# A fused attention + SwiGLU kernel: normalization of rows 5 to 7 reordered, one activation turn moved behind others, four transfers cut differently

## The chip, the cores and the metric

The kernel runs on one core of a Trainium2 chip. The metric is the device time of one execution in microseconds (us); the number given for a kernel is the median of several runs. The engines have short names in the profile: PE is the matrix engine (PEld its weight loads), DVE the vector engine, ACT the scalar engine, POOL the general one, and SP only issues transfers (its rows are SPq). Every engine works through its own list of instructions in order and waits on semaphores for the others. Transfers are issued by SP or ACT and carried by 16 DMA engines.

## The reference

Inputs are x (2048 tokens of 576 features), the attention weights wqkv (576 x 1728) and wo (576 x 576), and the feed-forward weights w_gate, w_up (576 x 4608) and w_down (4608 x 576), all bf16.

```python
xn = (x - mean(x)) / sqrt(var(x) + 1e-5)          # per token, over the 576 features
q, k, v = split(xn @ wqkv)                        # 32 heads of 18
# each token attends to itself and the 7 tokens 2, 4, ... 14 before it
attn = softmax over these 8 of (q . k) * 18**-0.5 # positions before the start get -1e9
o = sum over the 8 of attn * v
out = x + o @ wo + (silu(xn @ w_gate) * (xn @ w_up)) @ w_down
```

## The kernel before

**Tiling.** The 2048 tokens are seen as 16 rows of 128: partition p holds tokens 16p to 16p+15, and "row r" is the token r of every partition. A shift by 2 tokens is then mostly a shift by 2 rows on the same partition. The program has a first phase that makes q, k and v of the 16 rows, and then four token groups tt of four rows each, every one with nine chunks of gate and up matmuls (line 562) and the down and output projections (line 591). The attention itself is vector work, cut into pieces that a small planner (`Filler`) lays between the gate and up chunks.

**Names in the profile.** Several buffers share memory, and the profile prints the owner's name. The x rows (`xc_b`) and the normalized rows (`xn_b`, two buffers: rows 0-3 and 8-11 use the first, 4-7 and 12-15 the second) lie in the not yet needed `wd`, so `wd<-wd,mv,rstd` is a normalization. The qkv weights and the staged k and v (`stage`) lie in `hT`. `xnT` holds the normalized rows with the features on the partitions, which is what the matmuls read; "turning" a row means making its part of `xnT`.

**Normalizing a row** takes five steps: `ln_stats` (two BATCH_NORM_STATS2 and an aggregate on DVE, lines 210-211), `ln_sqrt` (ACT, 216), `ln_recip` (DVE, 221) and `ln_apply` (DVE, subtract and multiply at 226, and a copy of the last 64 features at 229, which a 64-row matmul needs twice). `ln_apply(8)` overwrites the place of row 0 and therefore waits until the transfer that turns row 0 has landed.

**Turning a row.** Rows 1 to 4 are turned on PE: `turn(r)` puts ten small transposing matmuls (263) into the matmul list of the row before, behind its 24th or 28th of 36 matmuls, and ACT and DVE each copy half of the result to `xnT` (267). Rows from 5 on are turned by a transposing transfer that SP issues (`transp_dma`, 271). Row 0 is needed in plain form at the very start and is turned a second time, as the others, by `transp_dma(0)` for the gate and up matmuls.

**The matmuls of a row** (`p_row`, 281) are 36, in 18 pairs of half-height tiles that run side by side, into four PSUM banks. `p_evac` copies the four banks out on ACT in six pieces (344); `between` puts an `ln_sqrt` before piece `last`. The banks of row r are used again by row r+2. Pieces 1, 2, 4 and 5 write `stage`; rows 8-11 write the buffers that rows 0-3 used, after SP's `move(0)` (356 to 359: halo copies into the rings `Kr` and `Vr`) has read them.

**Order on SP in the first phase:** loads, the two small ring fills (494), the turns of rows 5, 0, 6, 7, 8, 9, then `move(0)`, the turns of rows 10 to 13, `move(1)` with two `store`s, the turns of rows 14 and 15, then the second gate and up chunk. SP issues them strictly one after another. From row 4 on, the loop issues for each row r its matmuls, its evacuation, then `ln_sqrt`, `normalize` of rows 2r and 2r+1 and the statistics of the next two.

**The end.** Row 15 is the last output row. Its residual is added by a matmul, so its two halves are only copied from PSUM, one by ACT and one by DVE, and each engine's half is sent by a transfer of its own (606-607).

Of the kernel before, what the change touches and what calls it, by code (L numbers as in the profile page):

```python
# [20 lines left out]
HALF = D // 2  # L21
# [8 lines left out]
R = 16  # L30
RT = 4
# [39 lines left out]
def kernel(  # L71
# [11 lines left out]
    nc = tc.nc  # L83
# [6 lines left out]
    x_v = A_x.rearrange("b (p r) d -> p (b r) d", r=R)  # L90
    out_v = out.rearrange("b (p r) d -> p (b r) d", r=R)
# [26 lines left out]
    xr = big.tile([P, RT, D], bf16, name="xr")  # L118
    kv_d = dram.tile([2, NTT - 1, P, RT * D], bf16, name="kv_d")
# [3 lines left out]
    XC, XN = RT * D, RT * DPAD  # L123
# [9 lines left out]
    stage = [hTf[:, o + i * XC:o + (i + 1) * XC].rearrange("p (r d) -> p r d", d=D) for i in range(4)]  # L133
# [55 lines left out]
    def load_wd(ch):  # L189
        nc.sync.dma_start(wd[:, ch * FC:(ch + 1) * FC, :],  # L190
                          B_w_down[ch * FC * P:(ch + 1) * FC * P, :].rearrange("(f p) j -> p f j", p=P))
# [7 lines left out]
    def ln_open(c):  # L199
        mv = lns.tile([P, 4, 2], f32, name="mv")  # L200
        rstd = lns.tile([P, 4], f32, name="rstd")
        ln[c] = (xc_b[c], xn_b[c % 2], mv, rstd)

    def ln_stats(r, n=1):
        c, j = divmod(r, 4)
        xc, xn, mv, rstd = ln[c]
        for i in range(j, j + n):
            stats = lns.tile([P, 2, 6], f32, name="stats")
            for k in range(2):
                nc.vector.bn_stats(stats[:, k, :], xc[:, i, k * HALF:(k + 1) * HALF])  # L210
            nc.vector.bn_aggr(mv[:, i, :], stats[:].rearrange("p c s -> p (c s)"))  # L211

    def ln_sqrt(r, n=1):
        c, j = divmod(r, 4)
        xc, xn, mv, rstd = ln[c]
        nc.scalar.activation(rstd[:, j:j + n], mv[:, j:j + n, 1], ACT.Sqrt, bias=eps_t[:], scale=1.0)  # L216

    def ln_recip(r, n=1):
        c, j = divmod(r, 4)
        rstd = ln[c][3]  # L220
        nc.vector.reciprocal(rstd[:, j:j + n], rstd[:, j:j + n])

    def ln_apply(r, lo=0, hi=D):
        c, j = divmod(r, 4)
        xc, xn, mv, rstd = ln[c]
        nc.vector.tensor_scalar(xn[:, j, lo:hi], xc[:, j, lo:hi], mv[:, j, 0:1], rstd[:, j:j + 1],  # L226
                                op0=ALU.subtract, op1=ALU.mult)
        if hi == D:
            nc.vector.tensor_copy(xn[:, j, D:DPAD], xn[:, j, 512:D])  # L229
# [39 lines left out]
    def transp_dma(r):  # L269
        c, j = divmod(r, 4)  # L270
        nc.sync.dma_start_transpose(xnT[:, :, r * P:(r + 1) * P], ln[c][1][:, j, :])
# [12 lines left out]
    def p_row0(between):  # L284
        t = [new_ps("qkv_ps") for g in range(NG)]
        for kt in range(4):
            for g in range(NG):
                p_mm(t, g, kt, None, 0, kt == 0, False)
            if kt == 2:
                between()  # L290
        for i in range(2):
            for half in range(2):
                p_mm(t, i + 2 * half, 4, half, 0, False, True)
        return t
# [9 lines left out]
    def p_row(r, between=None, at=(0, 1)):  # L304


        t = [None] * NG
        fence = {}
        for swap in range(2):
            for i in range(2):  # L310
                kts = (0, 1, 2, 3) if swap else (0, 4, 1, 2, 3)
                for kt in kts:
                    for half in range(2):
                        g = i + 2 * (half ^ swap)
                        if t[g] is None:
                            t[g] = new_ps("qkv_ps")
                        mm = p_mm(t, g, kt, half, r, swap == 0 and kt == 0, swap == 1 and kt == 3)
                        if swap == 0 and kt == 3 and half == 1:
                            fence[i] = fence_after(mm)
                        if swap and kt == 0 and half == 0:  # L320
                            fence_before(mm, fence[i])
                    if swap and (i, kt) == at and between is not None:
                        between()
        return t

    def p_evac(r, t, only=range(6), between=None, last=6):


        c, j = divmod(r, 4)
        ks, vs = stage[2 * c % 4], stage[(2 * c + 1) % 4]  # L330
        vdst = vs[:, j, :].rearrange("p (d h) -> p d h", h=H)
        parts = [
            (QO[:, r, 0:G], t[0][:, 0:G]),
            (ks[:, j, HALF:D], t[2][:, 0:HALF]),
            (vdst[:, :, 0:8], t[2][:, HALF:G].rearrange("p (h d) -> p d h", d=DH)),
            (QO[:, r, G:D], t[1][:, 0:D - G]),
            (ks[:, j, 0:HALF], t[1][:, D - G:G]),
            (vdst[:, :, 8:H], t[3][:, 0:G].rearrange("p (h d) -> p d h", d=DH)),
        ]
        for n in only:  # L340
            if n == last:
                between()
            if r:
                nc.scalar.copy(*parts[n])  # L344
            elif n < 5:
                nc.scalar.mul(*parts[n], ln[0][3][:, 0:1])
            else:
                nc.vector.tensor_scalar(*parts[n], ln[0][3][:, 0:1], None, op0=ALU.mult)
# [9 lines left out]
        if c == 0:  # L358
            nc.sync.dma_start(ring[:, HALO:HALO + RT, :], st)

    def store(m, c):
        st = stage[(2 * c + m - 1) % 4]
        nc.sync.dma_start(kv_d[m - 1, c - 1], st.rearrange("p r d -> p (r d)"))

    def ring_load(m, tt):
        ring = Kr if m == 1 else Vr
# [85 lines left out]
    def normalize(r, n=1):  # L452
        ln_recip(r, n)
        for i in range(r, r + n):
            ln_apply(i)
            if i > 4:
                transp_dma(i)

    def turn(r):
        return lambda: transp_halves(r)  # L460
# [20 lines left out]
    t = p_row0(first)  # L481
# [6 lines left out]

    t = p_row(1, turn(2), (0, 3))
    ln_stats(3)  # L490
    p_evac(1, t, range(6), lambda: ln_sqrt(3), 4)
    normalize(3)
    for ring in (Kr, Vr):
        nc.sync.dma_start(ring[0:1, 0:HALO, :], wz[0:1, :].unsqueeze(1).to_broadcast([1, HALO, D]))

    t = p_row(2, turn(3))
    ln_open(1)
    ln_stats(4)
    p_evac(2, t, range(6), lambda: ln_sqrt(4), 3)
    normalize(4)  # L500
    ln_stats(5)

    t = p_row(3, turn(4))
    ln_sqrt(5)
    normalize(5)
    transp_dma(0)
    ln_stats(6, 2)
    p_evac(3, t)
    ln_sqrt(6, 2)
    normalize(6, 2)  # L510
    ln_open(2)
    ln_stats(8, 2)

    for r in range(4, R):
        t = p_row(r)
# [82 lines left out]
    def d_out(r, sub, t):  # L598
        ot = tmp.tile([P, D], bf16, name="ot", tag="ot", bufs=3)
        for h in range(2):  # L600
            cols = slice(h * HALF, (h + 1) * HALF)
            if r < R - 1:
                nc.vector.tensor_tensor(ot[:, cols], t[h][:, 0:HALF], xr[:, sub, cols], op=ALU.add)  # L603
                continue
            copy, eng = ((nc.scalar.copy, nc.scalar), (nc.vector.tensor_copy, nc.sync))[h]
            copy(ot[:, cols], t[h][:, 0:HALF])  # L606
            eng.dma_start(out_v[:, r, cols], ot[:, cols])
        if r < R - 1:
            nc.sync.dma_start(out_v[:, r, :], ot[:])

    for tt in range(NTT):
        for ch in range(NCH):
            it = tt * NCH + ch
            for p in range(2):
                g_pair(tt, ch, p)
                for j in (2 * p, 2 * p + 1):
                    g_evac(ch, j)
                    if it % NCH < NCH - 1 or p == 0:
                        dve.pump(1.4)
            if ch == NCH - 1:  # L620
                dve.drain(lambda: chains[0] > tt)
                for r in range(RT * tt, RT * tt + RT):
                    nc.sync.dma_start_transpose(oT[:, :, r * P:(r + 1) * P], QOP[:, r, :])
            if it + NSLOT < NTT * NCH:
                load_gu(it + NSLOT)
            if tt == 0:
                if 1 <= ch <= 7:
                    load_wd(ch - 1)
                for _ in range(3 if ch in (1, 2) else 2):
                    if wo_order:  # L630
                        load_wo(wo_order.pop(0))
                if ch == 0:
                    store(2, 3)
            if ch == 7:
                nc.sync.dma_start(xr[:], x_v[:, RT * tt:RT * tt + RT, :])
            if ch == 1 and tt < NTT - 1:
                chain(tt + 1)
        for sub in range(0, RT, 2):
            t, fence = {}, {}
            for swap in range(2):  # L640
                for i in (sub, sub + 1):
                    d_half(tt, i, swap, t, fence)
                    if swap:
                        dve.pump(12.5 if i == sub else 4.0)
                        d_out(RT * tt + i, i, t[i])
# [30 lines left out]
```

## Time and profile before

Three runs: 504.74 us median (504.69 to 504.84).

| what | value |
| --- | --- |
| time of the profiled execution | 504.91 us |
| its span, first to last instruction | 503.1 us |
| granted PE clock | 0.999 |
| PE busy | 497.4 us, 99% of the span |
| DVE busy | 328.8 us, 65% |
| ACT busy | 200.9 us, 40% |
| first phase, row matmuls (line 281) on the chain that ended last | 9% of the span |
| gate and up matmuls (562) on it | 56% |
| down and output matmuls (591) on it | 32% |

PE is the engine that sets the time: the chain that ended last runs through it for 96% of the span. Anything on another engine costs time only where PE has to wait for it, so the places to look for are the few short stretches in which PE is idle. The profiled execution is 0.17 us above the median of the runs.

### The profile page before, as it was taken

How to read it: one execution, taken by the hardware profiler on the slowest of the kernel's cores; microseconds unless marked ns; L12 is line 12 of the kernel's file. 1: busy time of each engine (PE TensorE's matmuls, PEld its weight loads, DVE VectorE, ACT ScalarE, POOL GpSimd, SP SyncE). 2: the span in 40 equal slices, each digit the busy share in tenths (PEclk: the TensorE clock that was granted, in tenths of full speed). 3: DMA queues.
4: the chain of work that ended last, by engine and by line, in shares of the span. 5: the costliest groups of instructions: out<-in, count | busy, mean ns of one | idle time of the engine just before them, and what ended most of it. 6: DMA issues, size and time to landing. Idle time of an engine off the chain costs nothing.

```text
span 503.1 us, 13262 instructions
## 1 busy us (share of the span) xinstructions
PE 497.4 (99%) x5799; PEld 283.4 (56%) x5799; DVE 328.8 (65%) x479; ACT 200.9 (40%) x416; POOL 0.7 (0%) x6
## 2 busy tenths in 40 slices
PE   8999999999999999999999999999999999999997
PEld 4555544444677644444777544445777444446775
DVE  5787598898999698999898139995980222221001
ACT  4756657754400255554300445557000444553000
POOL 0000000000000000000000000000000000000000
PEclk9999999999999999999999999999999999999999
DMA  8979988788921046536720054465500335553100
GB/s 311 251 198 247 293 293 272 227 266 261 236 88 61 25 129 200 187 104 228 150 85 38 28 185 149 135 189 156 136 25 14 107 113 172 166 165 40 27 14 25
DMA packets 76466, 75.42 MB, mean 150 GB/s; under 512 B 22628, under 2 KB 72192, under 8 KB 76408
## 3 DMA queue, kind: packets, MB, share of 16 engines
q1 hardware_dynamic: 75976, 73.91, 49.5%
q8 instruction: 45, 0.74, 0.6%
q10 hardware_dynamic: 432, 0.66, 0.4%
q14 instruction: 13, 0.11, 0.1%
HBM read 58.76 MB, written 5.90 MB: 129 GB/s over the span
## 4 chain that ended last, share of the span: by engine, by line
PE 96%; DMA 2%; DVE 1%; SPq 0%; ACT 0%; issue 0%
PE g_ps L562 56%; PE d_ps L591 32%; PE qkv_ps L281 9%; DMA hT<-in_A_wqkv_dram 1%; DMA xnT<-wd 1%; DVE stats L210 0%; DVE wd L226 0%; SPq L148 0%; ACT rstd L216 0%; PE pt L263 0%; DVE ot L606 0%; DVE mv L211 0%; ACT xnT L267 0%; SPq L144 0%; DVE wd L229 0%
## 5 line engine op out<-in xcount | busy, mean ns | idle before, releaser
L562 PE MATMUL g_ps<-xnT,gu 64*128 64x512 bf16 x2592 | 280.4, 376 | 0.0
L562 PEld LDWEIGHTS <-gu 64*128 64x128 bf16 x2592 | 126.1, 94 | 152.9
L573 ACT ACTIVATE sg<-g_ps 128x512 bf16<-128x512 f32 x144 | 87.3, 606 | 156.6 <-PE g_ps L562 156.6
L591 PE MATMUL d_ps<-wd,hT 64*128 64x288 bf16 x2304 | 146.4, 283 | 0.0
L591 PEld LDWEIGHTS <-hT 64*128 64x128 bf16 x2304 | 112.0, 94 | 29.8
L575 DVE TENSOR_TENSOR hT<-sg,uc 128x512 bf16<-128x512 bf16 x144 | 60.2, 419 | 93.5 <-ACT uc L574 93.2
L393 DVE TENSOR_REDUCE PP<-PP 128x64 f32<-128x1152 bf16 x64 | 84.9, 1347 | 0.4
L574 ACT CAST uc<-g_ps 128x512 bf16<-128x512 f32 x144 | 85.2, 592 | 0.0
L281 PE MATMUL qkv_ps<-hT,xnT 64*128 64x432 bf16 x540 | 50.3, 343 | 0.5 <-DMA xnT<-wd 0.5
L388 DVE TENSOR_TENSOR PP<-QO,Kr 128x2304 bf16<-128x2304 bf16 (+1 forms) x35 | 43.5, 1251 | 8.3 <-DMA Kr<-hT 8.1
L603 DVE TENSOR_TENSOR ot<-d_ps,xr 128x288 bf16<-128x288 f32 x30 | 12.3, 451 | 51.0 <-PE d_ps L591 51.0
L420 DVE TENSOR_TENSOR PP<-Vr,A 128x2304 bf16<-128x2304 bf16 (+1 forms) x35 | 43.3, 1251 | 0.4
L281 PEld LDWEIGHTS <-xnT 64*128 64x128 bf16 x540 | 26.7, 94 | 22.8 <-DMA xnT<-wd 1.2
L425 DVE TENSOR_TENSOR PP<-PP 128x2304 bf16<-128x2304 bf16 x24 | 32.5, 1354 | 0.3
L573 ACT ACT_TABLE_LOAD x5 | 6.4, 1283 | 47.2 <-PE g_ps L562 47.2
L591 PE MATMUL d_ps<-wo,xnT 64*128 64x288 bf16 x288 | 22.9, 283 | 0.0
L344 ACT CAST hT<-qkv_ps 128x288 bf16<-128x288 f32 (+2 forms) x60 | 21.9, 426 | 1.2 <-DMA Vr<-hT 0.8
L413 ACT ACTIVATE PP<-PP 128x1024 f32<-128x1024 f32 x4 | 4.2, 1057 | 31.3 <-DVE PP L409 31.2
L591 PEld LDWEIGHTS <-xnT 64*128 64x128 bf16 x288 | 14.0, 94 | 3.6
L606 ACT CAST ot<-d_ps 128x288 bf16<-128x288 f32 x1 | 0.4, 399 | 38.8 <-PE d_ps L591 38.8
L344 ACT CAST QO<-qkv_ps 128x432 bf16<-128x432 f32 (+1 forms) x30 | 12.4, 412 | 7.6 <-PE qkv_ps L281 7.6
L210 DVE BATCH_NORM_STATS2 stats<-wd 128x6 f32<-128x288 bf16 x32 | 12.8, 441 | 3.2 <-DMA wd<-in_A_x_dram 3.2
(48 smaller groups left out, 87.0 us busy)
## 6 DMA issues: line engine op xcount, KB each, us to landing
gu<-in_B_w_gate_dram SPq DMA_DIRECT2D x36, 512.0 KB, 3.8
gu<-in_B_w_up_dram SPq DMA_DIRECT2D x36, 512.0 KB, 5.1
wd<-in_B_w_down_dram SPq DMA_DIRECT2D x9, 576.0 KB, 5.9
kv_d<-hT SPq DMA_DIRECT2D x6, 576.0 KB, 5.7
gu<-in_B_w_gate_dram SPq DMA_DIRECT2D x36, 64.0 KB, 4.8
gu<-in_B_w_up_dram SPq DMA_DIRECT2D x36, 64.0 KB, 4.4
xr<-in_A_x_dram SPq DMA_DIRECT2D x4, 576.0 KB, 5.1
out_dram<-ot SPq DMA_DIRECT2D x15, 144.0 KB, 1.8
```

The lines of the kernel that those rows point to most:

```text
L210: nc.vector.bn_stats(stats[:, k, :], xc[:, i, k * HALF:(k + 1) * HALF])
L281: return nc.tensor.matmul(t[g][:, 0:G], xT_of(r)[rows, kt, :], w_at(g, kt, rows), start=start, stop=stop)
L344: nc.scalar.copy(*parts[n])
L388: nc.vector.tensor_tensor(prod[:, a:b], QO[:, RT * tt + a:RT * tt + b, :], Kr[:, s:s + b - a, :], op=ALU.mult)
L393: nc.vector.tensor_reduce(L[:, w, rs], prod[:, rs].rearrange("p r (h d) -> p r h d", d=DH), axis=AX.X, op=ALU.add)
L420: nc.vector.tensor_tensor(dst[:, a:b], Vr[:, s:s + b - a, :].rearrange("p r (d h) -> p r d h", h=H), A[:, w, a:b].unsqueeze(2).to_broadcas ...
L425: nc.vector.tensor_tensor(dst, acc, pv, op=ALU.add)
L562: mm = nc.tensor.matmul(ring_ps[j][b][:], gu[rows, slot, k, fc], xnT[rows, kt, tok], start=(swap == 0 and kt == 0), stop=(swap == 1 and kt ...
L573: nc.scalar.activation(sg[:], t[0][:], ACT.Silu)
L574: nc.scalar.copy(uc[:], t[1][:])
L575: nc.vector.tensor_tensor(hT[:, ch * FC + j, :], sg[:], uc[:], op=ALU.mult)
L591: mm = nc.tensor.matmul(t[sub][h][:, 0:HALF], a[rows], w[rows, h * HALF:(h + 1) * HALF], start=(swap == 0 and n == 0), stop=(swap == 1 and ...
```

## The change

Five edits, in the order of the program.

1. The statistics of row 4 go on DVE ahead of row 3's reciprocal and apply; the square root of row 3 goes one evacuation piece earlier on ACT, that of row 4 behind row 1's evacuation.
2. Row 4's apply and row 5's whole normalization move ahead of row 3's matmuls in the program; row 5's square root stands behind row 2's evacuation.
3. Rows 6 and 7 are normalized one at a time instead of as a pair, row 6's square root before the last piece of row 3's evacuation, row 7's behind it. `transp_dma(0)` now follows the turns of rows 6 and 7 on SP: the order is 5, 6, 7, 0, 8, 9.
4. `store(2, 3)` is sent as three transfers of 768 columns, and each load of `xr` (the x rows for the residual) as two transfers of two rows.
5. The last output row is one transfer of 576 columns from SP, which waits for both copies, in place of two of 288 from ACT and SP.

```diff
@@ normalization in the first phase
     t = p_row(1, turn(2), (0, 3))
     ln_stats(3)
-    p_evac(1, t, range(6), lambda: ln_sqrt(3), 4)
+    ln_open(1)
+    ln_stats(4)
+    p_evac(1, t, range(6), lambda: ln_sqrt(3), 3)
+    ln_sqrt(4)
     normalize(3)
...
     t = p_row(2, turn(3))
-    ln_open(1)
-    ln_stats(4)
-    p_evac(2, t, range(6), lambda: ln_sqrt(4), 3)
     normalize(4)
     ln_stats(5)
-
-    t = p_row(3, turn(4))
+    p_evac(2, t)
     ln_sqrt(5)
     normalize(5)
+
+    t = p_row(3, turn(4))
+    ln_stats(6)
+    p_evac(3, t, range(6), lambda: ln_sqrt(6), 5)
+    normalize(6)
+    ln_stats(7)
+    ln_sqrt(7)
+    normalize(7)
     transp_dma(0)
-    ln_stats(6, 2)
-    p_evac(3, t)
-    ln_sqrt(6, 2)
-    normalize(6, 2)
     ln_open(2)
     ln_stats(8, 2)
@@ store, and its call with parts=3
-    def store(m, c):
-        st = stage[(2 * c + m - 1) % 4]
-        nc.sync.dma_start(kv_d[m - 1, c - 1], st.rearrange("p r d -> p (r d)"))
+    def store(m, c, parts=1):
+        st = stage[(2 * c + m - 1) % 4].rearrange("p r d -> p (r d)")
+        n = XC // parts
+        for i in range(0, XC, n):
+            nc.sync.dma_start(kv_d[m - 1, c - 1, :, i:i + n], st[:, i:i + n])
...
-                    store(2, 3)
+                    store(2, 3, 3)
             if ch == 7:
-                nc.sync.dma_start(xr[:], x_v[:, RT * tt:RT * tt + RT, :])
+                for i in (0, 2):
+                    nc.sync.dma_start(xr[:, i:i + 2, :], x_v[:, RT * tt + i:RT * tt + i + 2, :])
@@ d_out, the last row
-            copy, eng = ((nc.scalar.copy, nc.scalar), (nc.vector.tensor_copy, nc.sync))[h]
-            copy(ot[:, cols], t[h][:, 0:HALF])
-            eng.dma_start(out_v[:, r, cols], ot[:, cols])
-        if r < R - 1:
-            nc.sync.dma_start(out_v[:, r, :], ot[:])
+            (nc.scalar.copy, nc.vector.tensor_copy)[h](ot[:, cols], t[h][:, 0:HALF])
+        nc.sync.dma_start(out_v[:, r, :], ot[:])
```

## The prediction

> **What bounds the kernel now.** I read the page's busy times first, then the chain of waits in order of time, then the single rows of the first 45 us. The busy times and the end of the chain:
>
> ```profile
> PE 497.4 (99%) x5799; PEld 283.4 (56%) x5799; DVE 328.8 (65%) x479; ACT 200.9 (40%) x416; POOL 0.7 (0%) x6
> ```
> ```profile
> 24.17 3.54 DMA xnT<-wd
> 27.75 33.02 PE qkv_ps L281 x360
> 60.78 69.93 PE g_ps L562 x648
> ...
> 459.57 39.98 PE d_ps L591 x652
> 499.55 0.45 DVE ot L606
> ```
>
> From 27.75 us to the last matmul PE never waits. So nothing can be gained there, and anything that stops PE there is lost in full. What can be gained lies before 27.75 and after 499.5. The pace gives the stalls: 33.02 us for 360 matmuls is 0.183 per pair, 3.29 per row of 18 pairs. In the listing of single matmul starts, pairs come 0.1825 apart except at these places of the stretch that the change touches: row 6 begins 0.80 behind the last pair of row 5 (26.95 to 27.75), so 0.62 is lost; row 5 begins 0.28 behind (0.09 lost). Both wait for a transposing transfer:
>
> ```profile
> PEld L281 <- DMA xnT<-wd: 1.2, 2, 0.9
> ACT hT L344 <- DMA Vr<-hT: 0.8, 1, 0.8
> ```
>
> The second line (ACT idle 0.8 us in front of row 8's evacuation, for the halo copy) matters below. Here is why row 6's turn was late. SP issues the turns of rows 5, 0 and 6 behind each other; row 0's took 4.5 us to land where others took 2.5 to 2.7, and row 6's stood behind it on the same engines. The stretches from 24.5 to 25.5, and SP's queue (start, length, what):
>
> ```profile
> 24.50:25.00 0.50, 0.50 (x10) 0.25 (x6) 0.48 (x3) 0.50 (x2) 0.00 (x0) 1.00 0.00 0
> 25.00:25.50 0.50, 0.50 (x10) 0.24 (x8) 0.47 (x3) 0.14 (x1) 0.00 (x0) 1.00 0.03 2
> ```
> ```profile
> 21.07 9.35 SPq L271 DMA_TRANSPOSE xnT<-wd  x6
> 30.51 0.58 SPq L356 DMA_DIRECT2D Kr<-hT  x1
> ...
> 34.30 0.83 SPq L359 DMA_DIRECT2D Vr<-hT  x1
> 35.24 5.74 SPq L271 DMA_TRANSPOSE xnT<-wd  x4
> ```
>
> In the last columns (DMA share, GB/s) no new data moves from 24.5 to 25.5, though two turns are under way. In those stretches the only other transfer is one 16 KB packet of the instruction queue, from 24.44 to 25.41; the held packets end together at 26.2. SP's rows show the other thing to keep in mind: from 27.89 to 40.98 SP issues without a pause, so a delay of row 8's turn is passed on to everything behind it, row 10's turn at 35.24 included.
>
> **The change part by part.**
>
> *Row 4's statistics ahead of row 3's normalization.* These DVE rows and the turn that needs them:
>
> ```profile
> 14.20 0.21 DVE L211 BATCH_NORM_AGGREGATE mv<-stats 128x2 f32<-128x12 f32 x1
> 14.77 0.16 DVE L221 RECIPROCAL rstd<-rstd 128x1 f32<-128x1 f32 x1 [0.36 <-ACT rstd L216]
> 14.97 0.43 DVE L226 TENSOR_SCALAR wd<-wd,mv,rstd 128x576 bf16<-128x576 bf16 x1
> 15.43 0.18 DVE L229 COPY wd<-wd 128x64 bf16<-128x64 bf16 x1
> ```
> ```profile
> 15.77 0.33 PE L263 MATMUL pt<-ident,wd 64*128 64x64 bf16 x10
> ```
>
> Row 4's statistics can start 0.13 behind that aggregate's start; two of them take 0.80 (21.92 to 22.72 for row 7) and their aggregate 0.13 until the next instruction starts. The 0.36 of waiting for ACT is filled with them; the rest delays the reciprocal from 14.77 to 15.25 and the copy's end from 15.61 to 16.10. PE's last pair of the turn ran at 15.89 without waiting; it will run at about 16.15. **PE loses 0.27.** It can't be nothing, since the copy ends behind the pair's old time; with the 0.11 from a DVE copy's end to the matmul start that row 2 shows (13.44 to 13.55) it is 0.35. The ACT square roots move into gaps, at no cost: row 3's waits for the aggregate at 14.41 as before.
>
> *Rows 4 to 7.* From the same spacings DVE ends row 4 at 17.67 (before 18.81), row 5 at 19.85 (21.04), row 6 at 22.72 (24.14), row 7 at 24.90 (24.70). Row 4's turn is then on time. Its DVE copy now stands behind row 5's normalization and ends near 20.3; row 4's matmuls want it at 20.44 + 0.27 = 20.71, so 0.3 of cover is left; without it, the wait is one for one. Row 5's turn is issued at 19.88, 1.2 earlier, behind loads that land until 23.13; even at its old 23.79 it is in time for 23.73 + 0.27 = 24.00. Row 6's is issued at 22.75 and even with row 0's 4.5 us lands at 27.25, for a need at 24.00 + 3.29 = 27.28. **The 0.62 and 0.09 go.** Row 7's square root now heads row 4's evacuation on ACT (23.92 instead of 23.23); its banks are wanted at 27.28 and free by 25.8: hidden.
>
> *Row 0's second turn behind row 7's.* It is issued when SP is through with row 7's, at 24.93 + 1.22 + 0.1 = 26.25 instead of 22.45. Row 8's apply overwrites row 0's place:
>
> ```profile
> 27.22 0.43 DVE L226 TENSOR_SCALAR wd<-wd,mv,rstd 128x576 bf16<-128x576 bf16 x1
> ```
>
> Before, row 0's turn landed at 26.98, just ahead of this apply. Now it lands between 26.25 + 2.5 and 26.25 + 4.8, the ends of all turns that have a landing. I take 2.6, the unobstructed rows, and 0.07 for a part chance that a blocked queue stretches row 7's issue from 1.22 to 1.67. With 0.2 from landing to a waiting DVE instruction, row 8's apply starts near 29.1, **1.9 late** (1.7 to 4.0). Behind it on DVE wait row 9's apply, the statistics of rows 10 and 11, and so ACT's next square root and evacuation; on SP the turns of rows 8 and 9, all six halo copies and the turns of rows 10 to 13.
>
> Who is hurt? Row 8's turn would land at 32.4 for a need at 33.85. Row 10's landed at 40.02 (issue 35.24 + 4.8), for a start at 40.89: it had 0.87 of cover. Now row 10 could start at 27.28 + 4 x 3.29 = 40.42, and its turn lands at 40.02 + 1.9 less what the halo copies catch up. They were held by an instruction packet at 36.11, in a full stretch; 1.9 later in their work they meet it with DMA shares of 0.78 to 0.98 left, room for 0.2. So it lands at 41.7 and row 10 starts at 41.77: **PE stalls 1.35**, 0.88 later than before. Row 8's evacuation, which waits for the halo copy (39.44 before, 41.1 then), frees row 10's banks at 41.5, just inside. Row 14's turn and banks keep over 1 us of cover. The attention pieces on DVE start up to 1.6 later, but end at 121 us for a need at 130.7.
>
> *Smaller transfers.* SP gets two more issues of about 0.4 at the store and one more per token group at `xr`. It waits for PE anyway, 4 us behind the store (72.3 to 76.4) and 1.7 in front of the output turns (129.1 to 130.7), so I take nothing; without that cover it is 0.8 and 0.4. POOL's list keeps its order.
>
> *Last output row.*
>
> ```profile
> out_dram<-ot SPq DMA_DIRECT2D x1, 144.0 KB, 1.7
> out_dram<-ot ACTq DMA_DIRECT2D x1, 72.0 KB, 1.9
> out_dram<-ot SPq DMA_DIRECT2D x1, 72.0 KB, 1.7
> ```
>
> Row 14's single transfer took 1.74 from issue to landing, others of that size up to 1.79. Issued at 500.03 it lands at 501.8; before, ACT's half landed last, at 501.92. **0.13 gained** (0 to 0.2). The Trainium skill (DMA: Bandwidth & Descriptors, Why this matters for kernel authors) has a fixed 2.0 us plus bytes over 436 GB/s, by which, as an estimate, 147 KB take 2.34 and either half 2.17: the merge would lose 0.17. By it the sum would be 0.3 higher; the rows here are all below its fixed part, so I go by the rows and give it no chance.
>
> Sum on the profiled time: 504.91 + 0.88 - 0.13 = 505.66. The profile stands 0.17 above the median, so the median comes to 505.5. The early stalls (+0.27, -0.71) drop out of this sum, since row 10's turn resets PE's clock.
>
> **The rivals.**
>
> 1. *Row 10's turn is in time.* If the instruction packet holds nothing up this time, the halo copies finish about 1.4 earlier, its turn lands near 40.4, and only the early terms count: +0.27 - 0.71 - 0.13 = -0.57, so 504.2. For it speaks that the packet must fall into a busy stretch; against, that it comes with PE's progress and falls into the copies again. The Trainium skill (Runtime: NRT & Kernel Launch, Instruction fetch mechanics) calls the cost of such a refill mostly hidden, which would make this the case; the empty stretch at 24.5 does not agree.
> 2. *Slower: row 0's turn is itself caught.* The packet at 24.44 moves to about 24.6, into row 6's turn, with rows 7 and 0 behind it. If row 0's landing takes 0.3 more than I took, the sum passes +1.0; at 0.7 more it is 505.5 + 0.7 = 506.2; at its old 4.5 us it would be 507.4.
> 3. *The early part does not do what it says,* row 6 still waiting. With row 10 late this changes nothing; alone with row 10 in time it gives 504.9.
>
> **How the numbers follow.** 0.2% is 1.0 us, about what a measurement of this kernel can tell from no change. The forecast case (505.1 to 505.75) has 0.44, rival 1 has 0.22, rival 2 has 0.30, rival 3 with row 10 in time 0.03, more than 0.2% faster 0.01: all that can be gained is 0.71 + 0.13 = 0.84, less than the bound. Rival 2 alone is beyond +0.2%, with a few of the forecast's: slower 0.31, same 0.68, faster 0.01. The range from 504.1 to 506.3 holds rival 1 and the nearer part of rival 2.
>
> **What would show it.** Right: no wait at row 6; PE waits near 40.4 to 41.8 for `xnT<-wd` or for ACT; DVE idle near 27.4 to 29 in front of line 226, for that turn; one output transfer landing in 1.75. Wrong: row 10 starting without a wait, DVE not idle at 27.4, or a PE gap beyond 45 us, where I have none.

## The result and the profile after

The changed kernel takes 506.49 us (median of 9 runs, 505.34 to 506.83), the kernel before 504.84 (9 runs, 504.17 to 506.05): slower by a ratio of 1.0029 [1.0019, 1.0040]. The forecast was 505.5 with a range up to 506.3, so the sign of the forecast's sum was right and its size too small. Profile against profile the difference is 506.17 - 504.91 = 1.26 us, for which the forecast was 0.75.

PE is still busy for nearly the whole span, with 0.9 us more of it than before (line references below are those of the changed kernel: gate and up matmuls are line 567 now, down and output 596, the last copies 610):

```profile
PE 498.3 (99%) x5799; PEld 284.4 (56%) x5799; DVE 328.7 (65%) x480; ACT 201.0 (40%) x417; POOL 0.7 (0%) x6
```

The list of waits of the changed kernel in its first 62 us (engine and line, what it waited for, us in total, times, longest):

```profile
ACT rstd L216 <- DVE mv L211: 11.9, 8, 3.8
...
PEld L281 <- DMA xnT<-wd: 2.5, 2, 1.9
DVE wd L226 <- DMA xnT<-wd: 2.3, 1, 2.3
...
PE qkv_ps L281 <- DMA xnT<-wd: 1.6, 2, 1.4
```

Before, the weight loads' wait for a turn was 1.2 in total, the longest of ACT for an aggregate 1.7, and the DVE line did not exist: row 8's apply never waited for a transfer. It now does, 2.3 us, as forecast. The timeline of DVE in the changed kernel has the place (start, length, what; in brackets the idle time in front and what ended it):

```profile
26.94 0.17 DVE L221 RECIPROCAL rstd<-rstd 128x2 f32<-128x2 f32 x1 [0.43 <-ACT rstd L216]
29.36 0.43 DVE L226 TENSOR_SCALAR wd<-wd,mv,rstd 128x576 bf16<-128x576 bf16 x1 [2.26 <-DMA xnT<-wd]
```

Before, this apply started at 27.22. It is 2.14 late. The chain that ended last, in order of time, runs through that wait where before it ran through row 6's turn and then PE alone:

```profile
25.35 0.55 SPq L271
...
25.95 3.31 DMA xnT<-wd
...
29.36 0.44 DVE wd L226
...
36.43 5.18 DMA Vr<-hT
41.63 0.28 ACT hT L344
...
50.18 5.55 DMA xnT<-wd
...
55.77 6.74 PE qkv_ps L281 x72
62.52 69.93 PE g_ps L567 x648
...
461.31 39.98 PE d_ps L596 x652
501.29 0.45 DVE ot L610
```

The row at 25.95 is row 0's second turn, 3.31 us from issue to landing; from there the chain stays off PE until row 14 starts at 55.77. From 62.52 on, the rest is the old sequence, only later (60.78 before). SP's list, on which the delay travels (the first row holds the turns of rows 5, 6, 7, 0, 8, 9; the last one those of rows 10 to 13):

```profile
19.54 13.01 SPq L271 DMA_TRANSPOSE xnT<-wd  x6
32.65 0.60 SPq L356 DMA_DIRECT2D Kr<-hT  x1
...
36.43 1.22 SPq L359 DMA_DIRECT2D Vr<-hT  x1
37.75 6.06 SPq L271 DMA_TRANSPOSE xnT<-wd  x4
```

Row 8's turn is issued at 30.03 (before 27.89, +2.14), row 10's at 37.75 (35.24, +2.51), row 14's at 50.18 (47.28, +2.90). The delay does not shrink on its way, it grows. On PE (start, length, what):

```profile
42.24 13.31 PE L281 MATMUL qkv_ps<-hT,xnT 64*128 64x432 bf16 x144 [1.43 <-DMA xnT<-wd]
55.77 6.74 PE L281 MATMUL qkv_ps<-hT,xnT 64*128 64x432 bf16 x72 [0.22 <-DMA xnT<-wd]
62.36 0.38 PE L567 MATMUL g_ps<-xnT,gu 64*128 64x512 bf16 x2
```

By the spacing from the first matmul of one pair to that of the next (0.1825 when nothing waits, 0.145 more for a turn on PE), the books from row 2 on are:

| place | lost before | lost after | forecast for after |
| --- | --- | --- | --- |
| row 3's turn on PE | 0 | 0.22 | 0.27 |
| row 5 | 0.11 | 0 | 0 |
| row 6 | 0.62 | 0 | 0 |
| row 9, wait until 37.37 | 0 | 0.36 | 0 |
| row 10, start at 42.24 | 0 | 1.76 | 1.35 |
| row 14, start at 55.77 | 0 | 0.38 | 0 |
| sum | 0.73 | 2.72 | 1.62 |

The net is 1.99, and the stretch from row 2's first matmul to the first gate matmul takes 2.01 longer (49.04 for 47.03). But row 2 starts 0.27 earlier in this profile (13.31 for 13.58), mainly because PE waited 0.5 less in row 0, ahead of anything that was changed. So the first gate matmul comes 1.74 later, at 62.36 instead of 60.62. Behind PE's last matmul the program needs 3.14 us to its end, 3.62 before: 0.48 gained. 1.74 - 0.48 = 1.26, the difference of the two profiled times.

### The profile page after: what moved, and what is told of

It reads as the page before. It is cut to its first block, busy times and chain, and to the rows that moved or that the text cites. A ratio compares the mean times of both kernels' runs of the same rounds, so it can differ in the third digit from the quotient of the medians.

```text
span 504.4 us, 13272 instructions
## 1 busy us (share of the span) xinstructions
PE 498.3 (99%) x5799; PEld 284.4 (56%) x5799; DVE 328.7 (65%) x480; ACT 201.0 (40%) x417; POOL 0.7 (0%) x6
## 4 chain that ended last, share of the span: by engine, by line
PE 91%; DMA 4%; DVE 2%; ACT 1%; SPq 1%; issue 0%; DVEq 0%
PE g_ps L567 55%; PE d_ps L596 32%; PE qkv_ps L281 4%; DMA xnT<-wd 2%; DMA Vr<-hT 1%; DVE stats L210 1%; DMA Kr<-hT 1%; DMA wd<-in_A_x_dram 1%; ACT hT L344 1%; ACT QO L344 0%; SPq L357 0%; DVE wd L226 0%; DVE PP L390 0%; PE pt L242 0%; SPq L356 0%
```

## The experiments

The theory (T): row 0's second turn lands too late for row 8's apply, which overwrites what that turn still reads; SP, saturated from row 8's turn on, passes the delay to the turns of rows 10 and 14. Against it stand three others: that the lateness comes from the reordered normalization, wherever row 0's turn is; that it comes from the smaller transfers; that row 10 is late by an instruction packet in its turn and not by the order. A further question was what made row 0's turn take 3.3 us.

**Row 0's turn put back between those of rows 5 and 6, all else as after (a_turn0_back).**

```diff
     ln_sqrt(5)
     normalize(5)
+    transp_dma(0)
...
     normalize(7)
-    transp_dma(0)
```

> The changed kernel with row 0's turn put back between the turns of rows 5 and 6; all other edits stay. Theory T (row 0's turn, landing late, holds row 8's apply and through it SP's whole list): row 8's apply starts without waiting near 27.1, row 10's turn lands near 40, no wait of PE at rows 9, 10 and 14; 504.84 - 0.7 (rows 5 and 6) + 0.2 (turn of row 3) - 0.1 to - 0.4 (last transfer) = 503.8 to 504.3 us. Theory U (the new order of the normalizations on DVE and ACT, or the smaller transfers, cost the time): stays at 506.2 to 506.7.

Measured: 504.00 us (11 runs, 503.64 to 504.36) against 504.87 for before, ratio 0.9975 [0.9963, 0.9987]. The wait of row 8's apply is gone. SP's list in this kernel:

```profile
19.53 10.79 SPq L271 DMA_TRANSPOSE xnT<-wd  x6
30.41 0.59 SPq L356 DMA_DIRECT2D Kr<-hT  x1
...
35.22 5.98 SPq L271 DMA_TRANSPOSE xnT<-wd  x4
```

Row 10's turn is issued at 35.22, as before (35.24), though rows 5 to 7 are normalized in the new way. PE loses 0.22 at row 3's turn, 0.13 at row 5, nothing at row 6, and 0.35 at row 10, where none was expected: row 10's turn took 5.30 here. So the reordered normalization is not the cause: 2.5 us between this kernel and after hang on one moved line.

**Only row 0's turn moved, in the kernel before (b_turn0_late).**

```diff
     normalize(5)
-    transp_dma(0)
...
     normalize(6, 2)
+    transp_dma(0)
     ln_open(2)
```

> The kernel before with only row 0's turn moved behind the turns of rows 6 and 7. Theory T: row 0's turn is issued near 26.7 and lands near 29.3 to 29.9, row 8's apply starts 2.3 to 2.9 late, row 6 no longer waits (0.6 gained), row 10 starts 1.7 to 2.2 later than before: 506.5 to 507.2 us. Theory U: only row 6's wait goes, 504.2.

Measured: 507.04 us (5 runs, 506.6 to 508.66), ratio 1.0045 [1.0030, 1.0061]. Row 0's turn runs from 26.73 to 29.71, row 8's is issued at 30.49, row 10's at 37.85. PE in this kernel:

```profile
29.66 11.60 PE L281 MATMUL qkv_ps<-hT,xnT 64*128 64x432 bf16 x116
43.03 5.28 PE L281 MATMUL qkv_ps<-hT,xnT 64*128 64x432 bf16 x56 [1.76 <-DMA xnT<-wd]
```

Row 10 starts at 43.03; 0.30, 0.36 and 2.09 us are lost at rows 8, 9 and 10. The moved line alone makes the kernel slower, by more than the whole change. With a_turn0_back this is T from both sides.

**The overwrite removed, the late turn kept (c_own_buffer).** Rows 8 to 11 are normalized into memory that is still free, the second slot of the gate and up weights, so no apply overwrites row 0.

```diff
-        ln[c] = (xc_b[c], xn_b[c % 2], mv, rstd)
+        xn = gu[:, 1].rearrange("p k n -> p (k n)")[:, 0:XN].rearrange("p (r d) -> p r d", d=DPAD) if c == 2 else xn_b[c % 2]
+        ln[c] = (xc_b[c], xn, mv, rstd)
```

> The changed kernel with the normalized rows 8 to 11 in a place of their own (the still empty second slot of the gate and up weights), so that row 8's apply has no transfer to wait for; SP's order is as in the changed kernel. Theory T: DVE doesn't wait at 27.1, row 8's turn is issued near 27.8 instead of 30.03, row 10's lands near 40; 503.9 to 504.6 us. Rival (not the overwritten place but row 0's turn in the transfer queue ahead of row 8's delays the chain): row 8's turn lands no earlier than 31.5, still above 505.5.

Measured: 504.05 us (11 runs, 503.62 to 504.62), ratio 0.9977 [0.9964, 0.9990]. DVE in this kernel, which writes row 8 to `gu`:

```profile
26.80 0.17 DVE L222 RECIPROCAL rstd<-rstd 128x2 f32<-128x2 f32 x1 [0.43 <-ACT rstd L217]
27.00 0.43 DVE L227 TENSOR_SCALAR gu<-wd,mv,rstd 128x576 bf16<-128x576 bf16 x1
27.46 0.18 DVE L230 COPY gu<-gu 128x64 bf16<-128x64 bf16 x1
```

No idle time stands in front of the apply, though row 0's turn lands at 29.52, later than in after (29.26). PE then runs rows 4 to 15 with one gap of 0.12:

```profile
19.16 40.81 PE L282 MATMUL qkv_ps<-hT,xnT 64*128 64x432 bf16 x444
```

So it is the place that row 8 overwrites, and not the turn's own traffic on SP or the DMA engines, that costs the time.

**The last output row alone, in the kernel before (d_end_one).**

```diff
-            copy, eng = ((nc.scalar.copy, nc.scalar), (nc.vector.tensor_copy, nc.sync))[h]
-            copy(ot[:, cols], t[h][:, 0:HALF])
-            eng.dma_start(out_v[:, r, cols], ot[:, cols])
-        if r < R - 1:
-            nc.sync.dma_start(out_v[:, r, :], ot[:])
+            (nc.scalar.copy, nc.vector.tensor_copy)[h](ot[:, cols], t[h][:, 0:HALF])
+        nc.sync.dma_start(out_v[:, r, :], ot[:])
```

> The kernel before with only the last output row sent as one transfer. From the profile of the changed kernel, 2.30 us from PE's end to its landing against 2.42, and 0.84 against 1.20 from there to the end of the span: 0.1 to 0.45 faster, 504.4 to 504.75 us. By the fit of the Trainium skill (DMA: Bandwidth & Descriptors), as an estimate, 0.17 slower.

Measured: 504.66 us (11 runs, 504.44 to 505.92), ratio 0.9989 [0.9972, 1.0007]. A gain of the end is not told from nothing by the times. In the profile PE's end to the end of the span is 3.30 us, 3.62 before. The end of this kernel, from the timeline:

```profile
499.51 0.46 DVE L605 CAST ot<-d_ps 128x288 bf16<-128x288 f32 x1 [4.19 <-PE d_ps L591]
499.55 0.40 ACT L605 CAST ot<-d_ps 128x288 bf16<-128x288 f32 x1 [38.77 <-PE d_ps L591]
500.03 0.33 SPq L606 DMA_DIRECT2D out_dram<-ot  x1
```

The one transfer is issued 0.55 behind PE's end, where SP's half was issued 0.52 behind it before: waiting for both copies costs it 0.04. It lands 2.28 behind PE's end, for 2.42 before, and from the landing to the end it is 1.02 for 1.20.

**The smaller transfers undone, in after (f_big_transfers).**

```diff
-                    store(2, 3, 3)
+                    store(2, 3)
...
-                for i in (0, 2):
-                    nc.sync.dma_start(xr[:, i:i + 2, :], x_v[:, RT * tt + i:RT * tt + i + 2, :])
+                nc.sync.dma_start(xr[:], x_v[:, RT * tt:RT * tt + RT, :])
```

> The changed kernel with the last store and the loads of xr in one piece again, as before. The prediction had these edits at nothing: 506.2 to 506.7 us, as the changed kernel. Rival (smaller transfers cost): 0.2 or more below the changed kernel.

Measured: 506.81 us (12 runs, 506.07 to 508.67), ratio 1.0034 [1.0020, 1.0048], not faster than after. PE loses 0.08, 0.36 and 1.98 at rows 8, 9 and 10. The splits cost nothing that shows, and are not the cause. They even gain a little at the end: from the last landing to the end of the span it is 1.02 us here, as in d_end_one, and 0.85 in after.

**The instruction packets moved, in after (e_fetch_moved).** Four of the large dummy matmuls that keep PE busy before the first data are replaced by 42 tiny ones, so PE's instruction list is longer ahead of the first phase and its refills come at other places of it. The computation is as before.

```diff
-    warm_pe(10, 1)
+    warm_pe(6, 1)
+    for _ in range(42):
+        nc.tensor.matmul(wp[0:32, 0:32], nc.const_aps.tensor(1.0, [P, 32], bf16), nc.const_aps.tensor(1.0, [P, 32], bf16),
+                         start=True, stop=True)
```

> The changed kernel with 42 tiny dummy matmuls in place of 4 of the 10 large ones at the start, where PE waits for x anyway. They do no work; they move PE's later instructions 76 places down, so that the 16 KB instruction packets of 23.66 and 37.36 us (changed kernel) come some 3.5 us earlier, near 20.2 and 33.9. Theory F (that packet holds a DMA engine and with it the transposing transfers): row 6's turn takes 2.6 instead of 4.0 us, row 0's lands 0.5 earlier, row 10's turn takes under 3.8 instead of 4.4 us; 504.7 to 505.6 us. Rival (the turns are late because they queue behind other transfers): row 10's turn again near 4.4 us behind its issue, 506.2 to 506.8.

Measured: 506.05 us (12 runs, 505.15 to 507.65), ratio 1.0014 [0.9997, 1.0031]: the median lies between the two expectations. The profiled execution is the fastest of the twelve, 505.15, so what the others lose beyond it is not seen. The 16 KB packets of the instruction queue that started at 23.66 and 37.36 in after start at 21.60 and 32.69 here. The stretches of this profile (start and end, their length, busy time of PE, PEld, DVE, ACT and POOL, granted clock, DMA share, GB/s; a packet is counted where it starts):

```profile
21.50:22.00 0.50, 0.50 (x10) 0.25 (x6) 0.46 (x2) 0.38 (x1) 0.00 (x0) 1.00 0.83 65
22.00:22.50 0.50, 0.50 (x10) 0.24 (x8) 0.47 (x3) 0.00 (x0) 0.00 (x0) 1.00 0.07 22
22.50:23.00 0.50, 0.50 (x8) 0.28 (x6) 0.50 (x2) 0.00 (x0) 0.00 (x0) 1.00 0.34 64
23.00:23.50 0.50, 0.50 (x10) 0.20 (x4) 0.28 (x2) 0.15 (x1) 0.00 (x0) 1.00 0.00 0
23.50:24.00 0.50, 0.25 (x4) 0.00 (x0) 0.29 (x2) 0.50 (x3) 0.00 (x0) 1.00 1.11 161
24.00:24.50 0.50, 0.00 (x0) 0.00 (x0) 0.47 (x3) 0.50 (x4) 0.00 (x0) 1.00 1.49 47
```

Row 5's turn is under way from 19.45 and row 6's from 22.38, yet little moves from 22.0 to 23.0 and nothing starts from 23.0 to 23.5, while the 16 KB packet takes from 21.60 to 23.86. Then PE stands, since row 5's turn lands only at 25.05 (5.6 us; 3.9 in after):

```profile
19.75 4.00 PE L281 MATMUL qkv_ps<-hT,xnT 64*128 64x432 bf16 x42
25.10 7.11 PE L281 MATMUL qkv_ps<-hT,xnT 64*128 64x432 bf16 x76 [1.35 <-DMA xnT<-wd]
```

Two turns became shorter: row 6's, now under the end of that packet, took 3.2 (4.0 in after), and row 0's, with no packet among its data, 2.65 (3.31). Row 9's became longer, 4.2 for 2.66, with the packet of 32.69 to 33.61 in it. PE lost nothing at rows 9, 10 and 14, being 1.5 late anyway. In this profile the delay goes where the packet goes. That row 10's turn would stay under 3.8 did not come true: without a packet in it, it still took 4.2 (4.45 in after), so the packet is not what makes that turn long, and row 10's lateness in after is SP's late issue at 37.75.

**What made row 0's turn 3.3 us long.** Stretches of after:

```profile
27.50:28.00 0.50, 0.50 (x8) 0.29 (x6) 0.00 (x0) 0.50 (x4) 0.00 (x0) 1.00 1.15 225
28.00:28.50 0.50, 0.50 (x10) 0.27 (x6) 0.00 (x0) 0.50 (x2) 0.00 (x0) 1.00 0.08 13
28.50:29.00 0.50, 0.50 (x10) 0.24 (x8) 0.00 (x0) 0.19 (x1) 0.00 (x0) 1.00 0.00 0
```

All packets of 256 B, the turn's data, have moved by 28.15. Its last two packets, of 4 B each, start at 28.47, just as an 8 KB packet of another instruction queue ends that ran from 27.90 to 28.47, and the landing is seen at 29.26. In e_fetch_moved that packet starts at 28.10, behind the turn's last data (27.99), and the turn lands at 28.45, 2.65 us from its issue. The same shows in five other profiles: with that packet falling into it row 0's turn took 3.29 (after_again), 3.33 (c_own_buffer), 3.31 (f_big_transfers) and 2.98 (b_turn0_late), and in d_end_one, where row 7's turn stood in its way, that one took 3.24 for 2.62 before. A packet at a turn's start did not do it: in a_turn0_back one ran from 27.87 to 28.38 and row 8's turn, issued at 27.79, took 2.57. It is argued from these, not shown: no run moved that packet alone.

**Is there more to gain: both cures, and none of the rest (h_own_late, i_own_late_stats, j_before_own_late, j_again).** h_own_late is c_own_buffer with row 0's turn behind those of rows 14 and 15:

```diff
     normalize(7)
-    transp_dma(0)
...
+        if r == 8:
+            transp_dma(0)
         if r == 9:
             load_gu(1)
```

> The changed kernel with the place of its own for rows 8 to 11, and row 0's turn, which nobody then waits for before 60 us, behind the turns of rows 14 and 15. Theory T: no wait at rows 9, 10, 14; rows 8 to 13 are turned some 1.2 us earlier on SP than with the own place alone; 503.6 to 504.2 us, at least as fast as with row 0's turn at its old place (504.0).

Measured: 504.31 us (12 runs, 503.75 to 508.11), ratio 0.9988 [0.9971, 1.0005]. Row 8's turn was not issued earlier than in c_own_buffer (27.67 there; 28.70 here, in a profile whose row matmuls start 0.75 later): in both it is issued as soon as DVE has row 8 ready (27.64 and 28.67), so SP held it up in neither. PE loses 0.09 at row 10. The expectation of 1.2 us earlier was wrong. i_own_late_stats is the same with row 4's statistics put back behind row 3's normalization:

```diff
-    ln_open(1)
-    ln_stats(4)
     p_evac(1, t, range(6), lambda: ln_sqrt(3), 3)
-    ln_sqrt(4)
     normalize(3)
+    ln_open(1)
+    ln_stats(4)
+    ln_sqrt(4)
```

> As the run before, with row 4's statistics behind row 3's normalization instead of ahead of it. PE's wait at row 3's turn (0.18 in the changed kernel) goes; row 3's copy on DVE stands behind the statistics and ends 0.28 later, with about 0.07 of a wait for it: 0.1 faster than that run, within what five rounds can tell.

Measured: 504.17 us (12 runs, 503.84 to 504.49), ratio 0.9980 [0.9968, 0.9991]. The loss at row 3's turn (0.22 by the spacing used here) is gone, but PE loses 0.27 at row 3's start, where 0.07 was expected, so the edit pays about nothing in either order. j_before_own_late is the kernel before with only these two cures, no reordered normalization:

```diff
-        ln[c] = (xc_b[c], xn_b[c % 2], mv, rstd)
+        xn = gu[:, 1].rearrange("p k n -> p (k n)")[:, 0:XN].rearrange("p (r d) -> p r d", d=DPAD) if c == 2 else xn_b[c % 2]
+        ln[c] = (xc_b[c], xn, mv, rstd)
...
     normalize(5)
-    transp_dma(0)
...
+        if r == 8:
+            transp_dma(0)
```

> The kernel before with the place of its own for rows 8 to 11 and row 0's turn behind the turns of rows 14 and 15; no normalization is reordered, no transfer cut differently, the end is as before. If row 0's turn in front of row 6's is all that held row 6: row 6's turn lands near 26.8 instead of 27.71, its wait of 0.62 goes, nothing waits at rows 9, 10 and 14; 504.85 - 0.6 = 504.1 to 504.4 us. If the reordering on DVE is needed for that gain: 504.7 to 504.9.

Measured: 505.15 us (11 runs, 504.14 to 505.74) against 505.1 for before on that chip, ratio 0.9992 [0.9976, 1.0008]: the median meets neither expectation. Its profiled execution took 504.14, and PE lost 0.12 in all behind row 4 in it: row 6's turn took 2.57 and was in time. It was run again:

> The same kernel as the run with row 0's turn last and nothing else changed, whose runs spread from 504.14 to 505.74 us: a second profile. If the spread comes from turns that land late in some executions, an execution above 505 us shows a wait of PE of 0.5 or more at one of the rows 5 to 14 for a transposing transfer; if it comes from the loads at the start, the row matmuls begin later and no wait lies between.

Measured: 504.48 us (8 runs, 504.07 to 505.12), ratio 0.9984 [0.9971, 0.9996], the profiled one again lowest (504.07, 0.15 lost). So the 0.62 that before loses at row 6 came from row 0's turn standing in front of row 6's, and goes without any reordered normalization; row 5 still loses 0.08. The profiled execution was below 505 us, so the question of that run was not answered: why the runs without a profile spread by 1 us upwards in this kernel stays open.

**The changed kernel again (after_again).** No edit.

> The changed kernel once more, for a second profile. Theory T: row 8's apply again waits for row 0's turn (2 us or more), row 10 again waits over 1 us; the smaller waits at rows 9 and 14 come and go with where the late transfers fall, their sum with row 10's stays at 2.0 to 2.5 us.

Measured: 506.47 us (8 runs, 506.17 to 506.69), ratio 1.0027 [1.0016, 1.0038], with 506.47 for the profiled execution. Row 0's turn took 3.29, row 8's apply waited 2.5, and PE lost 0.23, 0.36, 1.90 and 0.07 at rows 8, 9, 10 and 14: 2.55 in sum, 2.49 in the first profile, just above the 2.5 that was expected at most. The parts wander between the rows, the sum hardly does.

Three kernels are faster than before, with intervals wholly below 1: a_turn0_back (504.00), c_own_buffer (504.05) and i_own_late_stats (504.17). The kernel of j_before_own_late was so in its second measurement and not in its first. All these gains are under 0.3%.

## Why the prediction was right or wrong

**The place and the mechanism: right, and shown.** The turn of row 0 lands late, row 8's apply waits, SP passes it on, row 10's turn stops PE. Each link is in the profile of after; undoing the first (a_turn0_back) or cutting the second (c_own_buffer) takes the loss away, and doing the first alone (b_turn0_late) makes it. What failed is the size: the landing of row 0's turn and the catching up of the halo copies were mis-sized, and row 14's stall was left out.

**The step that failed first: "I take 2.6, the unobstructed rows".** Row 0's turn took 3.31 (3.29 in the repetition). Issued at 25.95 and not at 26.25, it let the apply start at 29.36, which is 2.14 late and not 1.9. The second rival had named this, a landing later than I took by 0.3 to 0.7, and priced the upper case at 506.2; 506.5 was measured. The range ended at 506.3 and so left out that rival's worse end. No run shows the 0.2 that the sum has from the landing to the waiting DVE instruction: it was 0.03 before (x landed at 3.78, DVE started at 3.81) and 0.10 here (29.26 to 29.36), which made the miss smaller.

**"Its turn lands at 40.02 + 1.9 less what the halo copies catch up": wrong in the second half.** They caught up nothing. From row 8's turn to row 10's, SP's delay grew from 2.14 to 2.51 (one halo issue took 1.22 where 0.83 was the price before), and the turn itself then took 4.45 for 4.78 before. So it landed 2.18 late, where the forecast had 1.68: 0.24 of the 0.50 from the apply, 0.26 from the catching up that did not happen. Row 10 started at 42.24 and not 41.77. PE was also 0.32 further ahead than forecast (row 6 started at 26.96, not 27.28), so the losses on the way to that start are 2.12 for 1.35: 1.76 at row 10 and 0.36 at row 9. At row 9 PE waited for a bank that ACT was late to empty: ACT's square roots stand ahead of the evacuations and waited for statistics that DVE had late (3.8 us in front of the one at 32.48), and row 7's evacuation freed the bank at 37.32, 0.05 ahead of the matmul that needs it. The prediction followed the delay on SP and named ACT's next square root and evacuation, but not the row that needs the bank. Row 10 was close to a wait for a bank too: row 8's evacuation got its halo copy at 41.63 (41.1 forecast) and freed the bank of row 10's second matmul at 41.91, only 0.3 ahead of the turn. With that turn alone in time, row 10 would have gained no more than that.

**"Row 14's turn and banks keep over 1 us of cover": wrong.** The cover was about that: row 14's turn took 5.55 from issue to landing here, so from 47.28 before it would have landed at 52.83, for a start at 27.75 + 8 x 3.29 = 54.07, cover 1.24. But that cover holds only if PE and SP are late alike, and the prediction gave no reason for it. Row 14 could have started 1.33 later than before, SP issued its turn 2.90 later, a difference of 1.57. It cost 0.38. A PE gap beyond 45 us was one of the prediction's signs of being wrong, and this is one. A delay on a saturated list has to be held against every later user of the list, not only the first.

**The early terms: right.** Rows 5 and 6 start without a wait. Row 3's turn cost 0.22 for 0.27. As forecast, none of this moves the end, since row 10 resets PE's clock. The first rival's 504.2, the case in which only the early terms count, is what a_turn0_back (504.00) and c_own_buffer (504.05) give.

**The end: a gain, but larger, 0.48 for 0.13.** From PE's end to the last landing it is 2.29 for 2.42, the 0.13 of the forecast; the single transfer took 1.74 to land, as forecast. The Trainium skill (DMA: Bandwidth & Descriptors, Anatomy of one DMA — SWDGE (gpsimd) path, which the prediction gave under a wrong section) would make it 2.34, as an estimate, and the merge a loss; its fit is stated for transfers issued by GpSimd, and for this one, issued by SP, the measured 1.74 decides. One row was misread as well: of the other whole-row transfers before, one took 3.45 and one 1.81, so "up to 1.79" is too low.

The other 0.35 is behind the landing, 0.85 for 1.20, and the prediction had no term for it. Before, SP goes through three more checks of semaphores there, some 0.065 apart; after, the last transfer's is the last that it checks. These checks are worth 0.17, and they go with the smaller transfers, not with the single one: d_end_one and f_big_transfers, which have the single transfer and not the splits, still have the three checks and take 1.02 from landing to end, and every kernel with both takes 0.84 or 0.85. The remaining 0.18 comes with the single transfer. In the kernels that send a half from ACT, ACT's last instruction but one takes 0.12 to 0.14, in the others 0.01, and POOL's next one follows it; that this makes the 0.18 is argued, not shown.

**The smaller transfers: no cost, as forecast** (f_big_transfers). The 0.17 that they gain at the end was not in the forecast.

The three differences close the books: 0.47 at row 10's start, 0.38 at row 14 and -0.35 at the end make 0.50, and the profiled times are 506.17 and, forecast, 505.66. The other half of the median's distance is the profile's place among the runs: after's first profile stood 0.32 under its median, where the forecast put it 0.17 above.

## What to carry to other kernels

When a transfer is moved later on a queue, ask first who overwrites what it reads: here the transfer's own result was not needed for over 30 us, and its source was needed at once. Where the queue behind it has no pause, carry the delay to every later user of that queue and hold it against each one's cover, and take the landing time of a transfer in a busy stretch from the obstructed rows as well, as one end of the range. Giving the new data another place cost nothing that shows here and took the loss away.

## What the runs showed of the hardware

- One packet on an instruction queue can hold up a whole transposing transfer. Such turns took 2.5 to 2.7 us where nothing fell into them, and row 5's took 5.6 (3.9 in after, behind the same loads) in e_fetch_moved with a 16 KB packet (2.26 us long) in it, during which the DMA share fell to 0.00; PE lost 1.51 there. Not every meeting costs: in j_again row 6's turn, issued at 24.01 under a 16 KB packet that ran from 23.62 to 24.93, took 2.57. By the Trainium skill (DMA: Bandwidth & Descriptors, Queues, rings and completion order) a DMA engine serves its rings in turn and changes only between whole packets; the two last packets of row 0's turn in after, which start at 28.47 as the 8 KB packet ends, agree. The Trainium skill (Runtime: NRT & Kernel Launch, Instruction fetch mechanics) calls the cost of such a refill mostly hidden; in this kernel, where matmuls wait for turns, it was not.
- The place of those packets follows PE's instruction list: 76 instructions more ahead of the first phase moved them from 23.66 to 21.60 and from 37.36 to 32.69, and a stall of 1.51 came up at row 5, while those at rows 9, 10 and 14 were gone. So a kernel's time can change by an edit that adds no work to the place where the time is lost.
- The order in which SP checks semaphores at the program's end counts: three checks behind the last landing, some 0.065 us apart, made 1.02 us from landing to end (d_end_one, f_big_transfers), and 0.85 with none (after).
